# Store of the gated values, places of the early down chunks, and order of work in the tail of a Fourier mixing and GEGLU kernel

## The chip, the cores and the metric

The kernel runs on one core of one Trainium2 chip. The metric is the device time of one execution in microseconds. The core has five instruction queues that run side by side and meet only through semaphores: PE (TensorE, matrix products), DVE (VectorE), ACT (ScalarE), POOL (GpSimd) and SP (SyncE, which here only issues DMA transfers). Each queue is worked through strictly in the order in which the kernel was written.

## The reference

Input x has 2048 rows of 448. Two blocks with residuals follow each other:

```python
h  = x + Re(DFT_seq(DFT_hidden(layernorm(x))))     # as products with cosine and sine matrices
g  = layernorm(h) @ w_gate                          # 448 -> 1792
u  = layernorm(h) @ w_up
h2 = h + (gelu(g) * u) @ w_down                     # 1792 -> 448
```

All inputs and outputs are float32.

## The kernel before

**Precision and products.** Every float32 operand is split into a high float16 half (ACT, `hi_part`, L108) and a low half, the rest (DVE, `lo_part`, L112 or L114). A product takes three float16 products: high by high, high by low, low by high. On top of that, two by two blocks are multiplied by Strassen's scheme with seven products instead of eight, so sums of blocks must be made before the split.

**Stages.** First come the Fourier products (up to about 340 us). Then 42 *units* of gate and up follow, one for each 128 columns of the hidden width and each block of rows: units 0 to 13 work on the first half of the rows (512-wide products), 14 to 27 and 28 to 41 on a quarter each (256-wide). From unit 14 on, the *down* product is woven in between. Down has 56 *chunks*: eight row parts p (0 to 7) of seven chunks n; chunk d is p = d // 7, n = d % 7. Each chunk is 21 products (seven of Strassen, three terms each) into the accumulators `acc_d[p]`. Units 14 to 41 hold chunks 0 to 41, one or two per unit (`COUNT`, L1375). Chunks 42 to 55 (p = 6 and 7) come after the last unit, in the *tail* (L1454 to L1496).

**A unit** (`GateUp`, L1027). PE does x1, z1, y1, x2, z2, y2, y3 into three PSUM banks X, Y, Z. DVE's `c12` reads Z behind z2; Z is then free for z1 of the next unit. ACT does the copies and the two GELUs; POOL multiplies one half of the gated values (L1104), and DVE makes the other half behind y3 (L1089). y3 of unit t-1 is done at the beginning of unit t. `store` (L1106) writes the gated values `hs` to memory (`hid_dram`): one store for each unit in units 0 to 13, one for each two units after that. `hs` has two buffers.

**Preparing a chunk.** `hid_load` (SP, L1127) brings the chunk's gated values back, into one of six buffers; it waits on SP until the store that wrote them has landed. `dn_sums` (POOL, L1174 and L1175) makes four Strassen sums, `dn_sum5` (DVE, L1179) the fifth, `dn_hi` (ACT) and `dn_lo` (DVE) the halves, each as one instruction for the 256 raw columns and one for the 640 columns of sums. The first six products of a chunk need the raw part only. For a chunk of the next unit, load is two units ahead; sums are made at the end of the unit before, the rest in the unit ahead of its use.

**Early chunks.** Eight chunks of the tail (42, 49, 43, 50, 44, 51, 45, 52: n = 0 to 3 of p = 6 and 7) are prepared inside the units; `EARLY` (L1133) maps a unit t to a chunk. Its load is in unit t-1, `dn_sums` at the end of t-1, `dn_sum5` and `dn_hi` in t, `dn_lo` in t+1. Chunks 42 and 49 use what units 28 and 29 stored, 43 and 50 units 30 and 31, 44 and 51 units 32 and 33, 45 and 52 units 34 and 35. The other six chunks (46, 47, 48, 53, 54, 55) are prepared in the tail, in the order of the list `jit` (L1461).

**Drain** (L926). When the seven chunks of a part p have been added up, ACT copies two banks (`copy`, L940), DVE adds the two others (`bank2`, `bank3`, L944), POOL does the eight sums of the copies (`sums`, L972), and SP stores the rows (`dn_store`, L1237). Part 6 has its accumulators in the banks X, tr, Z, Y; part 7 uses bank X again for its seventh Strassen sum, so chunk 49 needs part 6's first bank to be copied.

**What sets the order.** It is written out by hand. Around the change: the loop of units 0 to 13 (L1286), the loop of units 14 to 41 (L1383), and the tail.

Of the kernel before, what the change touches and what calls it, by code (L numbers as in the profile page):

```python
# [16 lines left out]
NF = DF // P  # L17
# [15 lines left out]
def kernel(  # L33
# [76 lines left out]
    def lo_part(dst, src, hi, scale=1.0):  # L110
        if isinstance(scale, float) and scale == 1.0:
            V.tensor_sub(dst, src, hi)  # L112
        else:
            V.scalar_tensor_tensor(dst, src, scale, hi, op0=ALU.mult, op1=ALU.subtract)  # L114
# [873 lines left out]
    NC = NF // 2  # L988
# [127 lines left out]
    def gw_load(t):  # L1116
        gw[t] = w_tile(f"gw{t}")
        nc.sync.dma_start(gw[t], w_dram[f_of(t)])
# [4 lines left out]
    def hid_load(d):  # L1123
        p, n = divmod(d, NC)
        hid_in[d] = fpool.tile([P, 4, P], F32, tag="hid", bufs=6, name=f"hid{d}")
        b = max(p // 2 - 1, 0)
        nc.sync.dma_start(hid_in[d], hid_dram[b, n][:, p % 2 if b else p])  # L1127

    def dn_hid(d):
        return hid_in[d]  # L1130

    LAST = range(6 * NC, 8 * NC)
    EARLY = dict(zip((32, 33, 35, 37, 38, 39, 40, 41), (42, 49, 43, 50, 44, 51, 45, 52)))  # L1133

    def dn_places():
        home = {}
# [23 lines left out]
    def dn_sums(d):  # L1160
        t = dn_hid(d)
        if d in LAST:
            spare.append(d)
            s = fops.tile([P, 5, P], F32, tag=("xn", "tt")[len(spare) % 2], name=f"dn_s{d}")
        elif d % 4 < 2:
            if d % 4 == 0:
                opened["l"] = late.tile([P, 10, P], F32, tag="dn_s", name=f"dn_s{d}")
            s = opened["l"][:, d % 4 * 5 :][:, :5]
        else:
            if d % 4 == 2:  # L1170
                opened["s"] = prep.tile([P, 10, P], F32, tag="s", name=f"dn_s{d}")
            s = opened["s"][:, d % 4 % 2 * 5 :][:, :5]
        dn_s[d] = s
        G.tensor_add(s[:, 0:2], t[:, 0:2], t[:, 2:4])  # L1174
        G.tensor_sub(s[:, 2:4], t[:, 1:4:2], t[:, 0:4:2])  # L1175

    def dn_sum5(d):
        t = dn_hid(d)
        V.tensor_add(dn_s[d][:, 4], t[:, 0], t[:, 3])  # L1179

    def dn_parts(d):
        return (dn_hid(d)[:, 0:4:3], slice(0, 2)), (dn_s[d], slice(2, 7))
# [6 lines left out]
    def dn_lo(d):  # L1189
        for src, dst in dn_parts(d):  # L1190
            lo_part(dn_w[d][:, 1, dst], src, dn_w[d][:, 0, dst])
# [44 lines left out]
    def dn_store(p):  # L1236
        nc.sync.dma_start(outr[p // 4, p % 4], hr[p])  # L1237
# [46 lines left out]
    prev = None  # L1284
    PREP_AT = {0: 0, 1: 1, 3: 2, 5: 3, 7: 4, 9: 5, 11: 6}
    for t in range(NF):  # L1286
        w = gu.get(t + 2) if t + 2 in JIT_F else None
        n = PREP_AT.get(t)
        if t > 0 and w is None:
            gw_load(t + 2)  # L1290
        if t + 2 == NF:
            for d in (0, 1, 2):
                hid_load(d)
        if t + 1 == NF:
            hr_load(0)
        if prev:
            prev.y3()
        if w:
            w.sums()
        if t == NF - 1:  # L1300
            dn_sum5(0)
        cur.y1()
        if t == 3:

            gelu_table()
        if w:
            w.hi(True)
        if n is not None:
            down_hi(n, 0)
            down_lo(n, 0)  # L1310
        cur.x2()
        if n is not None:
            down_hi(n, 1)
        if w:
            w.hi(False)
            w.lo(True)
        cur.z2()
        do(t, 1)
        cur.y2()
        do(t, 2)  # L1320
        cur.c_last()
        if t == NF - 1:
            dn_hi(0)
        if t == 1:
            hid_mm(NP - 1, 0)
        prev, cur = cur, GateUp(t + 1)
        cur.x1()
        if w:
            w.lo(False)
            gw[t + 2] = w.w  # L1330
        if n is not None:
            for part in W_LO1:
                down_lo(n, 1, part)
        if t + 1 in PREP_AT and t > 0:
            down_sums(PREP_AT[t + 1])
        if t == 0:
            down_sums(1)
        if t == NF - 1:
            dn_lo(0)
        cur.z1()  # L1340
        if t == 1:
            hid_mm(NP - 1, 1)
            hid_add(NP - 1, 0)
            ffn_moments(NB - 1, 1, hp[NB - 1, 1], 0)
            hid.close()
            late = ctx.enter_context(tc.tile_pool(name="late", bufs=1, reuse_waits="tile"))
            hops_tile(2)
        if t == 2:
            hid_add(NP - 1, 1)
            ffn_moments(NB - 1, 1, hp[NB - 1, 1], 1)  # L1350
            h_store(NB - 1, 1)

            sd_last = root(moments[NB - 1, 1], "h_last")
        if t == 3:
            mv = moments[NB - 1, 1]
            moments[NB - 1, 1] = mv, rstd(mv, sd_last, "h_last", const)
        if t == NF - 2:
            dn_sums(0)
        if t == NF - 1:
            dn_sums(1)  # L1360
            dn_sums(2)
        do(t, 3)
        if t > 0:
            before.store()
        before = prev
        if w:
            w.store()
        if w and w.f + 4 in JIT_F:
            gu[w.f + 4] = Weights(w.f + 4)
        if n is not None and 2 <= n + 2 < NC:  # L1370
            down_load(n + 2)
        do(t, 4)
# [3 lines left out]
    steps, d = {}, 0  # L1376
# [5 lines left out]
    drains, ended = {}, {}  # L1382
    for t in range(NF, N_GU):  # L1383
        now, ahead = steps[t], steps.get(t + 1, [])
        extra = EARLY.get(t)
        if t + 2 < N_GU:
            gw_load(t + 2)
        far = steps.get(t + 2, []) + ([EARLY[t + 1]] if t + 1 in EARLY else [])
        far += [46] if t + 1 == N_GU else []
        for d in far:  # L1390
            hid_load(d)
        for d in ahead:
            if d % NC == 0:
                hr_load(d // NC)
        if t in (N_GU - 4, N_GU - 2):
            hr_load(6 + (t == N_GU - 2))
        dn_mm(now[0], range(0, 6))
        prev.y3()
        for d in ahead:
            dn_sum5(d)  # L1400
        if t - 1 in EARLY:
            dn_lo(EARLY[t - 1])
        if t in EARLY:
            dn_sum5(EARLY[t])
        cur.y1()
        cur.x2()
        dn_mm(now[0], range(6, 13 if len(now) == 1 else 21))
        for d in ahead:
            dn_hi(d)
        cur.z2()  # L1410
        do(t, 1)
        cur.y2()
        cur.c_last()
        for d in ahead[:1]:
            dn_lo(d)
        if len(now) == 1:
            dn_mm(now[0], range(13, 21))
        else:
            dn_mm(now[1])
        if now[-1] % NC == NC - 1:  # L1420
            p = now[-1] // NC
            ended[p], drains[p] = t, dn_drain(p)
            drains[p].copy()
        prev = cur
        if t + 1 < N_GU:
            cur = GateUp(t + 1)
            cur.x1()
        if now[-1] % NC == NC - 1:
            drains[p].bank2()
            drains[p].bank3()  # L1430
        if t + 1 < N_GU:
            cur.z1()
        for d in ahead[1:]:
            dn_lo(d)
        for d in far:
            dn_sums(d)
        if extra is not None:
            dn_hi(extra)
        do(t, 2)
        do(t, 3)  # L1440
        if t == NF:
            before.store()
        if NF < t and t % 2 == 0:
            before.store()
        before = prev
        do(t, 4)
        for p, t0 in ended.items():
            if p < 5 and t - t0 in (1, 2):
                n = 4 * (t - t0)
                drains[p].sums(range(n - 4, n))  # L1450
            if p < 5 and t - t0 == 3:
                dn_store(p)
# [3 lines left out]
    prev.store()  # L1456
    hid_load(48)
    dn_sum5(46)
    dn_lo(52)
    drain = drains[5]  # L1460
    jit = [46, 47, 48, 53, 54, 55]  # L1461
    for i, d in enumerate(range(6 * NC, 7 * NC + 4)):
        dn_mm(d)
        if jit:
            n = jit.pop(0)
            dn_hi(n)
            if jit:
                dn_sums(jit[0])
            dn_lo(n)
            if jit:  # L1470
                dn_sum5(jit[0])
            if len(jit) > 2:
                hid_load(jit[2])
            if i == 0:
                drain.sums(range(8))
                dn_store(5)
        if d == 7 * NC - 1:
            drain = dn_drain(6)
            drain.copy()
            drain.bank2()  # L1480
            drain.bank3()
            drain.sums(range(8))
            dn_store(6)

    drain = Drain(hr[7], (), (), 1.0 / (H_SC * W_SC))
# [71 lines left out]
```

## Time and profile before

| | |
|---|---|
| median of 3 runs | 719.24 us (718.64 to 721.21) |
| the profiled execution | 717.73 us, of it span from first to last instruction 716.0 us |
| TensorE clock granted | 1.000 |
| busy in the span | PE 704.2, DVE 522.1, ACT 355.5, POOL 201.9 us |
| DMA | 160.47 MB, mean 224 GB/s, 74.8% of 16 engines' time |
| unit 33 begins | 611.79 us |
| the tail's first chunk (42) begins | 679.51 us |
| PE's last product ends | 712.75 us |

A timeline row reads: start in us, duration in us, engine, line, operation, output<-inputs, shape and count of merged instructions, and in brackets how long the engine sat idle just before and what released it. A row of waits reads: waiting engine, tile and line, then what released it, us in total, times, longest. A row of a stretch reads: from:to, its length, and for PE, PE's weight loads, DVE, ACT and POOL the busy us with the count of instructions; then the clock, DMA's share and GB/s. A row of a group reads: line, engine, operation, count, and the shortest, median and longest duration in ns.

### The profile page before, as it was taken

The page shows a single profiled execution, that of the slowest core. Times are in us where ns is not written, and L with a number is a line of the kernel's source. Part 1 is how long each engine was busy: PE and PEld are TensorE (multiplying, and loading weights), DVE is VectorE, ACT ScalarE, POOL GpSimd, SP SyncE. Part 2 cuts the span into 40 slices and gives each one's busy share as a digit, 9 for nine tenths or more (in the row PEclk, how much of TensorE's full clock was granted, in tenths as well). Part 3 has the DMA queues.
Part 4 walks back from the last instruction along what each step waited for, and adds up shares of the span by engine and source line. Part 5 has one row for each costly group of instructions (what it writes and reads, how often), then busy time and mean ns, then how long its engine had stood idle before and what let it go on. Part 6 is the DMA issues. An engine that isn't in the chain of part 4 may idle for free.

```text
span 716.0 us, 13066 instructions
## 1 busy us (share of the span) xinstructions
PE 704.2 (98%) x4952; PEld 480.7 (67%) x4952; DVE 522.1 (73%) x1024; ACT 355.5 (50%) x656; POOL 201.9 (28%) x240
## 2 busy tenths in 40 slices
PE   9999999999999999999999999999999999999986
PEld 6555555555555555897644444469999999899986
DVE  7997638486858679998648777456777765978974
ACT  5776524162526444543527565455555544546530
POOL 0000000000000000000213333344485756678982
PEclk9999999999999999999999999999999999999999
DMA  7787629999998969652836858797798976879431
GB/s 270 248 248 263 146 104 243 232 310 246 225 308 245 250 212 238 238 136 91 222 123 204 314 188 194 225 293 244 219 287 267 274 253 208 295 252 321 165 116 51
DMA packets 116463, 160.47 MB, mean 224 GB/s; under 512 B 62000, under 2 KB 80560, under 8 KB 116400
## 3 DMA queue, kind: packets, MB, share of 16 engines
q1 hardware_dynamic: 116400, 159.64, 74.8%
q8 instruction: 38, 0.62, 0.3%
q14 instruction: 25, 0.20, 0.1%
HBM read 110.85 MB, written 34.87 MB: 204 GB/s over the span
## 4 chain that ended last, share of the span: by engine, by line
PE 92%; DVE 4%; POOL 1%; DMA 1%; issue 1%; ACT 0%; SPq 0%; ACTq 0%; POOLq 0%; DVEq 0%
PE acc L648 33%; PE pY L1010 13%; PE acc_d L1219 12%; PE y L714 9%; PE pX L1010 9%; PE pZ L1010 9%; PE acc_f L520 7%; DVE dn_w L112 1%; DMA hid_dram<-hs 1%; DVE dn_s L1179 1%; POOL hr L972 1%; PE pw L102 1%; DVE dn_l L112 0%; ACT dn_w L108 0%; DVE hr L944 0%
## 5 line engine op out<-in xcount | busy, mean ns | idle before, releaser
L648 PE MATMUL acc<-xs,ws 128*128 128x448 f16 x1248 | 237.9, 352 | 0.0
L648 PEld LDWEIGHTS <-ws 128*128 128x128 f16 x1248 | 122.1, 98 | 113.8
L1010 PEld LDWEIGHTS <-gw 128*128 128x128 f16 x1365 | 133.4, 98 | 44.6 <-issue 1.7
L1219 PE MATMUL acc_d<-wd,dn_w 128*128 128x224 f16 x1008 | 111.3, 259 | 2.9 <-DVE dn_w L112 2.3
L220 POOL TENSOR_TENSOR wd_s<-wd 128x448 f32<-128x448 f32 x7 | 9.5, 1352 | 343.4 <-DMA wd<-in_w_down_dram 342.6
L1219 PEld LDWEIGHTS <-dn_w 128*128 128x128 f16 x1008 | 96.6, 98 | 5.8 <-DVE dn_w L112 3.2
L1010 PE MATMUL pY<-hops,gw 128*128 128x256 f16 (+1 forms) x595 | 89.9, 294 | 0.0
L1104 POOL TENSOR_TENSOR hs<-hs,c 128x256 f32<-128x256 f32 (+1 forms) x42 | 47.5, 1131 | 127.6 <-DVE hs L1020 64.4
L114 DVE SCALAR_TENSOR_TENSOR ws<-wr,ws 128x1024 f16<-128x1024 f32 (+2 forms) x66 | 75.0, 1139 | 9.3 <-ACT ws L108 8.9
L108 ACT ACTIVATE ws<-wr 128x1024 f16<-128x1024 f32 (+2 forms) x66 | 63.8, 980 | 21.7 <-DMA wr<-in_w_seq_dram 20.5
L714 PE MATMUL y<-wh,z 128*128 128x448 f16 x336 | 66.2, 352 | 0.0
L1010 PE MATMUL pZ<-hops,gw 128*128 128x256 f16 (+1 forms) x385 | 61.7, 294 | 1.2 <-DVE c L1020 1.2
L1010 PE MATMUL pX<-hops,gw 128*128 128x256 f16 (+1 forms) x385 | 61.7, 294 | 0.0
L112 DVE TENSOR_TENSOR dn_w<-dn_s,dn_w 128x640 f16<-128x640 f32 x48 | 55.5, 1156 | 5.8 <-ACT dn_w L108 5.6
L1174 POOL TENSOR_TENSOR dn_s<-hid 128x256 f32<-128x256 f32 x56 | 45.4, 812 | 29.2 <-DMA hid<-hid_dram 27.9
L714 PEld LDWEIGHTS <-z 128*128 128x128 f16 x336 | 32.9, 98 | 30.1
L520 PEld LDWEIGHTS <-ws 128*128 128x128 f16 x504 | 48.3, 98 | 0.9
L1010 PEld LDWEIGHTS <-gu_w 128*128 128x128 f16 x273 | 26.6, 98 | 31.9 <-issue 0.2
L1066 ACT ACTIVATE u<-pY 128x256 f32<-128x256 f32 (+1 forms) x42 | 19.1, 455 | 57.6 <-PE pY L1010 57.5
L1175 POOL TENSOR_TENSOR dn_s<-hid 128x256 f32<-128x256 f32 x56 | 46.2, 826 | 0.0
L108 ACT ACTIVATE dn_w<-dn_s 128x640 f16<-128x640 f32 x48 | 35.1, 730 | 21.4 <-DVE dn_s L1179 10.1
L1089 DVE SCALAR_TENSOR_TENSOR hs<-pY,g 128x256 f32<-128x256 f32 (+1 forms) x42 | 21.3, 506 | 33.5 <-PE pY L1010 33.0
(133 smaller groups left out, 909.7 us busy)
## 6 DMA issues: line engine op xcount, KB each, us to landing
gw<-w_dram SPq DMA_DIRECT2D x35, 896.0 KB, 5.7
wr<-in_w_seq_dram SPq DMA_DIRECT2D x100, 256.0 KB, 4.7
hid_dram<-hs SPq DMA_DIRECT2D x28, 512.0 KB, 7.1
hid<-hid_dram SPq DMA_DIRECT2D x56, 256.0 KB, 5.9
w_dram<-gu_w SPq DMA_DIRECT2D x14, 896.0 KB, 5.4
gu_raw<-in_w_gu_dram SPq DMA_DIRECT2D x28, 384.0 KB, 5.9
wr<-in_w_seq_dram SPq DMA_DIRECT2D x14, 512.0 KB, 5.2
x<-in_x_dram SPq DMA_DIRECT2D x16, 224.0 KB, 2.9
```

The costliest lines, as they stand in the source:

```text
L108: A.activation(dst, src, AF.Copy, scale=scale)
L112: V.tensor_sub(dst, src, hi)
L114: V.scalar_tensor_tensor(dst, src, scale, hi, op0=ALU.mult, op1=ALU.subtract)
L520: PE.matmul(fast_sum(n, k), fast_a(n, i, lw, a), fast_b(j, lx, b), start=j == 0 and m == 0 and k % 2 == 0, stop=j == NT // 2 - 1 and m == ...
L648: PE.matmul(acc[key][:, :D], w[:, lw, block * P : (block + 1) * P], xs[c][:, lx, :], start=c == 0 and m == 0, stop=c == NT - 1 and m == 2,)
L714: PE.matmul(y[:, :D], z[p][:, lz, k, g * P : (g + 1) * P], wh[:, lw, k, :], start=k == 0 and m == 0, stop=k == 6 and m == 2,)
L1010: PE.matmul(ps, w[:, wl, wa + ws, :], ops[:, m + ms, :], start=first and n == 0, stop=last and n == len(terms) - 1, skip_group_check=True,)
L1089: V.scalar_tensor_tensor(h, y, SC, g, op0=ALU.mult, op1=ALU.mult)
L1104: G.tensor_mul(c22, c22, self.cols(self.c12))
L1174: G.tensor_add(s[:, 0:2], t[:, 0:2], t[:, 2:4])
L1175: G.tensor_sub(s[:, 2:4], t[:, 1:4:2], t[:, 0:4:2])
L1219: PE.matmul(ps, w[:, la, a, :], wd[n][:, lb, b, :], start=n == 0 and m == 0 and opens, stop=n == NC - 1 and m == 2, skip_group_check=True,)
```

## The change

Three things. The store of the gated values is issued right behind y3 and its product, at the beginning of the next unit, instead of near that unit's end. The eight early chunks are placed in units 32 to 39 without gaps. In the tail, low halves of chunk 52 are gone (they now fall into unit 40); the chunks still to be prepared are tied to the tail's iterations 0, 1, 2, 3, 7 and 8, with 54 and 55 behind drain 6's copy; drain 5's eight POOL sums are split into four in iteration 0 and four in iteration 2; the last three loads are all issued in iterations 0 to 2; drain 6's POOL sums and store move two iterations back.

```diff
-    EARLY = dict(zip((32, 33, 35, 37, 38, 39, 40, 41), (42, 49, 43, 50, 44, 51, 45, 52)))
+    EARLY = dict(zip(range(32, 40), (42, 49, 43, 50, 44, 51, 45, 52)))
...
@@ units 0 to 13
         if prev:
             prev.y3()
+            prev.store()
...
         do(t, 3)
-        if t > 0:
-            before.store()
-        before = prev
...
@@ units 14 to 41
         prev.y3()
+        if t % 2 == 0:
+            prev.store()
...
         do(t, 3)
-        if t == NF:
-            before.store()
-        if NF < t and t % 2 == 0:
-            before.store()
-        before = prev
...
@@ tail
     dn_sum5(46)
-    dn_lo(52)
-    drain = drains[5]
-    jit = [46, 47, 48, 53, 54, 55]
+    jit = {0: (46, 47), 1: (47, 48), 2: (48, 53), 3: (53, 54), 7: (54, 55), 8: (55, None)}
     for i, d in enumerate(range(6 * NC, 7 * NC + 4)):
         dn_mm(d)
-        if jit:
-            n = jit.pop(0)
+        if i in jit:
+            n, after_n = jit[i]
             dn_hi(n)
-            if jit:
-                dn_sums(jit[0])
+            if after_n:
+                dn_sums(after_n)
             dn_lo(n)
-            if jit:
-                dn_sum5(jit[0])
-            if len(jit) > 2:
-                hid_load(jit[2])
-            if i == 0:
-                drain.sums(range(8))
-                dn_store(5)
-        if d == 7 * NC - 1:
+            if after_n:
+                dn_sum5(after_n)
+        if i < 3:
+            hid_load(53 + i)
+        if i in (0, 2):
+            drains[5].sums(range(2 * i, 2 * i + 4))
+        if i == 2:
+            dn_store(5)
+        if i == NC - 1:
             drain = dn_drain(6)
             drain.copy()
             drain.bank2()
             drain.bank3()
+        if i == NC + 1:
             drain.sums(range(8))
             dn_store(6)
```

## The prediction, made before the changed kernel was run

> **What bounds the kernel now.** I read the page's busy times, then the waits of PE, then the order in time around each wait, then busy time by unit.
>
> ```profile
> span 716.0 us, 13066 instructions
> PE 704.2 (98%) x4952; PEld 480.7 (67%) x4952; DVE 522.1 (73%) x1024; ACT 355.5 (50%) x656; POOL 201.9 (28%) x240
> ...
> PE acc_d L1219 <- ACT v L940: 3.1, 1, 3.1
> PE acc_d L1219 <- DVE dn_w L112: 2.3, 2, 1.4
> ...
> PE pZ L1010 <- DVE c L1020: 1.2, 3, 0.6
> PE acc_d L1219 <- ACT dn_w L108: 0.4, 1, 0.4
> ```
>
> PE is the bound: 716.0 - 704.2 leaves 11.8 us in which it idles, and no reordering can return more. The four named waits shown make 7.0 us of that. Where they lie decides. The tail, in order of time:
>
> ```profile
> 679.51 4.19 PE L1219 MATMUL acc_d<-wd,hops 128*128 128x224 f16 x42
> ...
> 683.53 2.17 PE L1219 MATMUL acc_d<-wd,dn_l 128*128 128x224 f16 x21
> ...
> 684.52 6.02 POOL L972 TENSOR_TENSOR hr<-hr,v 128x224 f32<-128x224 f32 x8
> ...
> 691.93 0.74 ACT L108 ACTIVATE dn_w<-dn_s 128x640 f16<-128x640 f32 x1 [4.61 <-POOL dn_s L1175]
> ...
> 692.70 1.25 DVE L112 TENSOR_TENSOR dn_w<-dn_s,dn_w 128x640 f16<-128x640 f32 x1 [4.53 <-ACT dn_w L108]
> ...
> 694.00 1.42 PE L1219 MATMUL acc_d<-wd,dn_w 128*128 128x224 f16 x13 [0.91 <-DVE dn_w L112]
> ...
> 695.26 1.89 PE L1219 MATMUL acc_d<-wd,hops 128*128 128x224 f16 x18
> ...
> 699.00 0.74 ACT L108 ACTIVATE dn_w<-dn_s 128x640 f16<-128x640 f32 x1 [1.29 <-DVE dn_s L1179]
> ...
> 699.65 0.96 ACT L940 ACTIVATE v<-acc_d 128x448 f32<-128x448 f32 x2
> ...
> 700.22 0.45 PE L1219 MATMUL acc_d<-wd,hops 128*128 128x224 f16 x3 [3.08 <-ACT v L940]
> ...
> 706.55 6.20 PE L1219 MATMUL acc_d<-wd,dn_w 128*128 128x224 f16 x63
> ```
>
> Two chains. First, POOL adds all eight sums of drain 5 (6.02 us) before the two sums of chunk 48; ACT's high half and DVE's low half follow, and PE waits 0.40 + 0.91 us in chunk 48. Second, PE stops after 18 products of chunk 49, whose seventh sum goes into bank X; that bank is free only when drain 6's copy (699.65) has read it, and ACT does the copy behind the high half of chunk 55 (699.00). PE waits 3.08 us.
>
> Units 33 to 41 (rows: PE, PEld, DVE, ACT, POOL busy in a stretch that is one unit):
>
> ```profile
> 611.79:618.86 7.07, 6.44 (x63) 5.83 (x60) 6.93 (x15) 4.61 (x11) 5.19 (x7) 1.00 0.99 348
> ...
> 627.14:633.41 6.27, 6.27 (x62) 5.83 (x60) 4.39 (x8) 3.69 (x9) 6.27 (x10) 1.00 0.72 259
> ...
> 641.69:647.96 6.27, 6.27 (x62) 5.82 (x60) 4.55 (x8) 4.46 (x11) 5.04 (x7) 1.00 1.00 350
> ...
> 656.25:663.07 6.82, 6.43 (x62) 5.82 (x60) 5.50 (x10) 4.61 (x11) 6.74 (x10) 1.00 0.91 340
> 663.07:671.67 8.60, 8.44 (x83) 7.84 (x81) 8.60 (x12) 4.86 (x12) 8.60 (x10) 1.00 0.55 193
> 671.67:679.51 7.84, 7.69 (x77) 7.08 (x74) 7.78 (x12) 3.06 (x9) 6.83 (x8) 1.00 0.39 125
> ```
>
> A one-chunk unit takes 6.27 us undisturbed. Unit 33 takes 0.80 more, unit 39 0.55 more; unit 40 (two chunks: 21 products more, 6.27 + 2.01 = 8.28) 0.32 more, and unit 41 (42 products of down and, without x1 and z1 of a next unit but with its own y3, 32 of its own at 0.109: 7.52) 0.32 more, a hole at its head: 1.99 us in all. They are the units in which DVE or POOL has no room.
>
> **Part one: the earlier store.** A store on SP waits for its data and holds what is behind it, so SP's order counts. In the code, what lies between the old and the new place on SP is, unit by unit: nothing, except in unit 2, where the store passes the store of h. The transposes and dn_store stand behind the old place already; loads of gw, hid and hr ahead of the new one. So it is nearly the same queue. The one wait that a store causes shows why it stays:
>
> ```profile
> 462.70 8.74 SPq L306 DMA_TRANSPOSE hops<-xs  x3
> ...
> 472.65 0.54 SPq L1110 DMA_DIRECT2D hid_dram<-hs  x1
> ...
> 480.19 0.42 DVE L1020 SCALAR_TENSOR_TENSOR hs<-pY,m 128x256 f32<-128x256 f32 x1 [2.91 <-DMA hid_dram<-hs]
> ...
> 481.00 0.56 PE L1219 MATMUL acc_d<-wd,dn_w 128*128 128x224 f16 x4 [1.40 <-DVE dn_w L112]
> ```
>
> The store of unit 12 issues at 472.65 because three transposes from the end of iteration 12 hold SP to 471.4; both places of the store are in iteration 13, behind them. Price 0. Bounds: 0 and -1.40 (that wait gone). If unit 2's swap had no cover (PE idles nowhere there), it would cost one 0.5 us issue.
>
> **Part two: the tail.** PE does 14 chunks of 21 products = 294 from 679.51 to 706.55 + 6.20 = 712.75: 33.24 us. The first two rows give 42 in 4.02 (start to start): 0.0957 each, so 28.1, and 0.16 for the last to drain: 28.3. So 4.9 us can go: 4.39 of waits and about 0.5 of restarts. Does it? After, POOL does four of drain 5's sums (3.0 us) instead of eight before chunk 48, and copy 6 has only the high half of chunk 53 before it. Chunk 52's low half is no longer in the tail (two DVE instructions fewer at its head). What remains ahead of chunk 48 is a round trip through memory:
>
> ```profile
> 680.88 0.32 SPq L1114 DMA_DIRECT2D hid_dram<-hs  x1
> ...
> 684.21 0.79 SPq L1127 DMA_DIRECT2D hid<-hid_dram  x2
> ...
> DMA to landing us min/median/max: 2.7/3.4/3.8
> ...
> DMA to landing us min/median/max: 2.7/5.7/7.6
> ...
> DMA to landing us min/median/max: 3.0/7.0/8.1
> ```
>
> (The last rows, of the views by tile and by line: loads of hid from 670 on; loads of hid from 580 on; stores of hid from 590 on.) The store landed in 3.3 us, the load in 2.7: chunk 48 is there at 686.9, or 687.6 with the 0.7 us of part three. POOL has done sums 46, 47 and four of drain 5 by about 686. Then POOL 1.44, ACT 0.74, DVE 1.3: 691.1. PE asks for that half at 680.2 + 6 x 2.01 + 0.6 = 692.8: 1.7 us of slack. Copy 6: chunk 48 ends at 694.3, bank X is copied by 694.9, asked for at 696.0. Its eight POOL sums follow chunk 55's and end near 702, before PE's end at 708.5. Price -4.9; bounds -4.9 and, if 48's chain is late as now, -3.4 (the 3.08 and its restart alone).
>
> **Part three: early chunks in units 32 to 39.** Chunk 43 moves up by one unit, and 50, 44, 51, 45, 52 by two each. Nothing is added over all; the room changes. DVE works strictly in order: y3's product, fifth sums of the chunks ahead, low halves of the last early chunk, fifth sum of the new one, and only then c12, which frees bank Z for the next unit's z1. Unit 39 shows the whole list:
>
> ```profile
> 657.57 0.42 DVE L1089 SCALAR_TENSOR_TENSOR hs<-pY,g 128x256 f32<-128x256 f32 x1 [1.87 <-PE pY L1010]
> ...
> 661.95 0.41 DVE L1020 SCALAR_TENSOR_TENSOR c<-pZ,u 128x256 f32<-128x256 f32 x1
> ...
> 662.42 0.82 PE L1010 MATMUL pZ<-hops,gw 128*128 128x256 f16 x6 [0.39 <-DVE c L1020]
> ```
>
> y3 is ready 1.32 us into the unit; the list takes 4.38 to c12. z1 is the last 6 of 39 products of 0.109, due at 656.25 + 5.61 = 661.86, and starts 0.56 late. Now units 33 and 39 have this list with two chunks ahead (and 40). After, 33, 35, 37 and 39 have it: 0.80 + 3 x 0.5 = 2.3. Add a low half of the next chunk that comes late at a unit's head, as the 0.32 at unit 41, and copy 4 in unit 37 behind a late c12: 0.5 together. Units 40 and 41 lose their 0.64, since chunk 45's fifth sum and low halves leave them. 2.8 against 1.99: **+0.8**. Units 36, 38 and 40, with one chunk more of PE work, ask for c12 2.0 us later; walked through with the rows below, DVE reaches it 0 to 0.8 us in time.
>
> ```profile
> L1174 POOL TENSOR_TENSOR dn_s<-hid x26: 718/738/1306, 589.7 to 679.7; 128x256 f32<-128x256 f32 x26
> ...
> L1179 DVE TENSOR_TENSOR dn_s<-hid x25: 279/808/842, 592.6 to 677.4; 128x128 f32<-128x128 f32 x25
> L112 DVE TENSOR_TENSOR dn_w<-dn_s,dn_w x18: 810/1278/1352, 588.5 to 674.0; 128x640 f16<-128x640 f32 x18
> ```
>
> ```profile
> L112 DVE TENSOR_TENSOR dn_w<-hid,dn_w x26: 407/415/950, 581.2 to 698.8; 128x256 f16<-128x256 f32 x26
> ```
>
> These are the same instructions with and without POOL at work beside them: a pair of low halves is 1.22 or about 2.2 us. Bounds: -1.2 (only unit 33 still waits) and +2.1 (units 36 and 38 each late by one contended pair's extra 1.0 as well).
>
> Each early load now follows its store by one unit instead of up to three, and SP waits for the store's landing.
>
> ```profile
> 609.48 0.37 SPq L1114 DMA_DIRECT2D hid_dram<-hs  x1
> ```
>
> For chunk 43: 609.5 + 7.0 + 5.7 (the medians) = 622.2; DVE comes to it at 624.1. Behind the load on SP stand only hr and the next gw, due a unit later. At the longest of both (8.1 and 7.6), 625.2: 1.1 us of DVE, about what unit 34 has to spare before z1 of unit 35.
>
> **Sum.** 717.73 (its span 716.0 and 1.73 around it) - 4.9 + 0.8 + 0 = 713.6. The median shown, 719.24, lies 1.5 above the profiled execution; carried to it: 719.24 - 4.1 = **715.1**.
>
> [...]
>
> [...]
>
> **Rivals and chances.** Forecast (tail whole, units +0.3 to +1.5), 714.6 to 715.8: 0.50. Units cost nothing or gain (to -1.2), 713.1 to 714.6: 0.16; for it speaks DVE's idle in units 35 and 37 (4.39 and 4.55 of 6.27). DVE's lag carries over through unit 37's drain into 38 (+2.1 to +3), 716.4 to 717.3: 0.20; for it, six full units in a row. Chunk 48's round trip at the medians above (7.0 and 5.7 instead of 3.3 and 2.7): 6.7 later less 1.7 slack, 5.0 lost, 720.1: 0.05; against it the light traffic there. Full exclusion, 720.6: 0.04. Part one does reach SP's order and the 1.40 goes, 713.7: 0.05. That it does nothing is in the forecast.
>
> About 0.5% (3.6 us: below 715.6) is what a measurement of this kernel tells from no change, and the forecast lies only just outside. Faster: most of the first case, the second and the last, 0.58; slower by as much (above 722.8): 0.04; within: 0.38. Range 712.9 to 717.8; it leaves out the two slow cases and part of the carry-over.
>
> **What would show it.** Right: no wait of PE on ACT v, copy 6 straight behind chunk 48, POOL's drain 5 in two halves, PE's last product about 4 us earlier; PE waits on c12 in units 33, 35, 37, 39 of about 0.5; the 1.40 at 481 unchanged. Wrong: a wait on hid loads on DVE in units 34 to 38, a wait over 1 us in unit 38, or a stop in chunk 48.

## The result, and the profile after

| | before | after |
|---|---|---|
| median of five executions, in turn | 719.24 us (718.37 to 721.21) | 715.19 us (713.94 to 716.42) |
| the profiled execution | 717.73 us | 716.42 us |
| its span | 716.0 us | 714.6 us |
| its TensorE clock | 1.000 | 0.998 |
| first product of unit 32 | 605.52 us | 604.96 us |
| the tail's first product | 679.51 us | 683.09 us |
| units 32 to 41 | 73.99 us | 78.13 us |
| the tail, to PE's last product | 33.24 us | 28.34 us |

The ratio is 0.994, with an interval of 0.9917 to 0.9964: 4.05 us faster by the medians. The two profiled executions differ by only 1.3 us, since that of before was quicker than its five executions and that of after is the slowest of its own. Both have a reason, which the experiments found and the prediction had not seen.

The busy times of the changed kernel and what PE waited for:

```profile
PE 705.7 (99%) x4952; PEld 481.6 (67%) x4952; DVE 526.4 (74%) x1024; ACT 355.4 (50%) x656; POOL 203.3 (28%) x240
```

```profile
PE pZ L1010 <- DVE c L1020: 3.2, 4, 1.9
PE pw L102 <- POOL sign_t L93: 1.4, 1, 1.4
PE acc_d L1219 <- DVE dn_w L112: 1.1, 2, 0.9
```

The 3.08 us on ACT's copy are gone, and so is the stop in chunk 48. The waits on `c12` have grown from 1.2 to 3.2 us. The tail in order of time:

```profile
683.09 4.19 PE L1219 MATMUL acc_d<-wd,hops 128*128 128x224 f16 x42
...
684.62 0.32 SPq L1114 DMA_DIRECT2D hid_dram<-hs  x1
684.72 3.39 POOL L972 TENSOR_TENSOR hr<-hr,v 128x224 f32<-128x224 f32 x4
...
689.00 1.74 SPq L1127 DMA_DIRECT2D hid<-hid_dram  x4
...
691.14 6.20 PE L1219 MATMUL acc_d<-wd,dn_w 128*128 128x224 f16 x63
691.62 0.42 ACT L108 ACTIVATE dn_w<-hid 128x256 f16<-128x256 f32 x1 [3.19 <-DMA hid<-hid_dram]
...
694.16 1.25 DVE L112 TENSOR_TENSOR dn_w<-dn_s,dn_w 128x640 f16<-128x640 f32 x1 [1.39 <-ACT dn_w L108]
...
696.82 0.53 ACT L940 ACTIVATE v<-acc_d 128x448 f32<-128x448 f32 x1
...
697.18 2.18 PE L1219 MATMUL acc_d<-wd,hops 128*128 128x224 f16 x21
...
705.23 6.20 PE L1219 MATMUL acc_d<-wd,dn_w 128*128 128x224 f16 x63
```

PE works from 683.09 to 705.23 + 6.20 = 711.43 with no bracket behind any of its rows: 28.34 us, where 28.3 was forecast. The copy (696.82) is done before chunk 49, from 697.18 on, asks for its bank. Chunk 48 is a closer call. Its low half is complete at 694.16 + 1.25 = 695.41; PE comes to the sums part of it at 697.18 - 2.01 + 0.6 = 695.77. That is 0.36 us of slack.

The units cost more than forecast. Rows of units 33 to 41 (columns as in the prediction's rows of stretches; the last three of a row are clock, DMA share and GB/s):

```profile
611.23:618.25 7.02, 6.43 (x63) 5.82 (x61) 6.88 (x15) 4.62 (x11) 5.21 (x7) 1.00 0.95 351
618.25:626.53 8.28, 8.28 (x84) 7.84 (x81) 8.28 (x12) 3.92 (x10) 6.12 (x8) 1.00 0.85 270
626.53:633.29 6.76, 6.43 (x63) 5.82 (x60) 5.59 (x10) 4.58 (x11) 6.76 (x9) 1.00 0.80 285
633.29:641.96 8.67, 8.45 (x83) 7.77 (x81) 8.67 (x12) 3.96 (x10) 8.67 (x11) 1.00 0.42 129
641.96:650.46 8.50, 6.60 (x62) 5.75 (x60) 6.75 (x12) 5.00 (x12) 6.17 (x8) 1.00 0.94 331
650.46:660.48 10.02, 9.95 (x83) 8.71 (x81) 8.67 (x16) 4.55 (x12) 6.50 (x8) 0.83 0.85 284
660.48:667.29 6.81, 6.42 (x62) 5.82 (x60) 5.49 (x10) 4.61 (x11) 6.38 (x10) 1.00 0.85 292
667.29:675.58 8.29, 8.29 (x84) 7.83 (x82) 8.29 (x12) 4.87 (x12) 8.29 (x10) 1.00 0.31 123
675.58:683.09 7.51, 7.51 (x76) 7.16 (x74) 4.08 (x8) 2.96 (x7) 2.33 (x4) 1.00 0.41 131
```

Units 40 and 41 lost their lateness, as the prediction had it (8.29 and 7.51 against its 8.28 and 7.52). Units 33, 35 and 39 are 0.5 to 0.75 over 6.27, unit 36 is 0.39 over 8.28. Two are far off. Unit 37 is 8.50 instead of 6.27. Unit 38 is 10.02 instead of 8.28, and PE is *busy* in 9.95 of it, at a mean clock of 0.83. What led to both, in order of time:

```profile
633.48 4.05 POOL L972 TENSOR_TENSOR hr<-hr,v 128x224 f32<-128x224 f32 x4
...
637.55 0.39 SPq L1237 DMA_DIRECT2D out_dram<-hr  x1
...
638.03 0.42 SPq L1118 DMA_DIRECT2D gw<-w_dram  x1
...
638.54 1.88 SPq L1127 DMA_DIRECT2D hid<-hid_dram  x3
...
644.69 0.29 DVE L1179 TENSOR_TENSOR dn_s<-hid 128x128 f32<-128x128 f32 x1 [0.97 <-DMA hid<-hid_dram]
...
645.76 0.63 DVE L1179 TENSOR_TENSOR dn_s<-hid 128x128 f32<-128x128 f32 x1 [0.78 <-DMA hid<-hid_dram]
...
649.65 0.81 PE L1010 MATMUL pZ<-hops,gw 128*128 128x256 f16 x6 [1.90 <-DVE c L1020]
...
651.21 2.55 PE L1010 MATMUL pY<-hops,gw 128*128 128x256 f16 x11
```

SP stands at the store of drain 3 (L1237) until POOL has finished that drain's sums, at 637.5. Behind it in SP's queue are the weights of unit 38 and three loads: chunks 35 and 36, which unit 38 uses, and the early chunk 51. Before, the same store went out 2.27 us sooner:

```profile
631.79 3.46 POOL L972 TENSOR_TENSOR hr<-hr,v 128x224 f32<-128x224 f32 x4
...
635.28 0.39 SPq L1237 DMA_DIRECT2D out_dram<-hr  x1
```

So in unit 37 DVE finds the two chunks not yet landed and stands 0.97 + 0.78 = 1.75 us. `c12` follows late by about as much, and z1 of unit 38 waits 1.90 us. About 1.3 us after that wait the clock falls to half:

```profile
649.50:652.00 2.50, 2.28 (x16) 1.81 (x16) 2.47 (x6) 2.37 (x7) 1.12 (x3) 0.80 0.85 296
652.00:654.00 2.00, 2.00 (x12) 1.39 (x11) 1.90 (x5) 0.55 (x2) 2.00 (x3) 0.50 0.50 99
654.00:656.00 2.00, 2.00 (x20) 1.87 (x19) 2.00 (x5) 1.20 (x4) 1.50 (x2) 0.90 0.88 358
```

The three rows lack 2.50 x 0.20 + 2.00 x 0.50 + 2.00 x 0.10 = 1.7 us of full clock: 3.4 us at half. y1 of unit 38, eleven products, takes 2.55 us there and 1.36 elsewhere. The account of the profiled pair closes: 0.56 us less up to unit 32 (most of it the wait near 480, now 0.89 instead of 1.40), 4.14 more in units 32 to 41, 4.90 less in the tail, 0.08 less behind PE: 1.4 less in the span.

### The profile page after: what moved, and what is told of

It is laid out like the page before. It is cut to its first block, busy times and chain, and to the rows that moved or that the text cites. A ratio compares the mean times of both kernels' runs of the same rounds, so it can differ in the third digit from the quotient of the medians.

```text
span 714.6 us, 13070 instructions
## 1 busy us (share of the span) xinstructions
PE 705.7 (99%) x4952; PEld 481.6 (67%) x4952; DVE 526.4 (74%) x1024; ACT 355.4 (50%) x656; POOL 203.3 (28%) x240
## 4 chain that ended last, share of the span: by engine, by line
PE 93%; DVE 3%; DMA 2%; issue 1%; ACT 0%; SPq 0%; POOL 0%; POOLq 0%; DVEq 0%
PE acc L648 33%; PE acc_d L1219 14%; PE pY L1010 13%; PE y L714 9%; PE pZ L1010 8%; PE pX L1010 8%; PE acc_f L520 7%; DMA hid_dram<-hs 1%; DMA hid<-hid_dram 1%; DVE dn_s L1179 1%; DVE dn_w L112 1%; PE pw L102 1%; DVE hops L112 0%; DVE dn_l L112 0%; ACT dn_w L108 0%
## 5 line engine op out<-in xcount | busy, mean ns | idle before, releaser
L1104 POOL TENSOR_TENSOR hs<-hs,c 128x256 f32<-128x256 f32 (+1 forms) x42 | 45.8, 1091 | 129.7 <-DVE hs L1020 81.9
L1174 POOL TENSOR_TENSOR dn_s<-hid 128x256 f32<-128x256 f32 x56 | 48.1, 859 | 30.5 <-DMA hid<-hid_dram 30.5
L1175 POOL TENSOR_TENSOR dn_s<-hid 128x256 f32<-128x256 f32 x56 | 45.8, 817 | 0.0
L972 POOL TENSOR_TENSOR hr<-hr,v 128x224 f32<-128x224 f32 x56 | 45.3, 835 | 0.6
```

Source lines behind the costliest of these rows:

```text
L972: op(x, x, m)
L1104: G.tensor_mul(c22, c22, self.cols(self.c12))
```

## The experiments

My theory: the tail brings the gain by two separate chains (chunk 48's sums on POOL, the copy on ACT); the earlier store brings nothing; the new places of the early chunks cost time, because DVE comes late to `c12` in the units with a full list and because SP is held in unit 36. The rivals: the earlier store carries some of the gain; the copy alone makes the tail; the cost of the places is spread evenly and has nothing to do with SP. Each kernel was run in turn with the kernel before, whose median beside them lay at 719.13 to 719.76 us. e1 to e4 ran on one chip, e5 to e8 on a second, e9 to e12 on a third, so between these groups the ratios are the better comparison.

| kernel | median, us | ratio to before | interval |
|---|---|---|---|
| e1: tail alone | 713.43 | 0.9912 | 0.9894 to 0.9930 |
| e2: early places alone | 719.36 | 0.9997 | 0.9984 to 1.0010 |
| e3: store alone | 719.23 | 1.0001 | 0.9986 to 1.0017 |
| e4: changed kernel, drain's rows stored a unit later | 714.16 | 0.9930 | 0.9911 to 0.9949 |
| e5: changed kernel again | 714.55 | 0.9932 | 0.9914 to 0.9950 |
| e6: e1, two transposes later | 716.98 | 0.9963 | 0.9946 to 0.9979 |
| e7: early chunks in even units, two more in the tail | 722.57 | 1.0036 | 1.0020 to 1.0052 |
| e8: e1, copy behind 54 and 55 | 720.65 | 1.0010 | 0.9999 to 1.0021 |
| e9: e1, one transpose later | 712.52 | 0.9904 | 0.9887 to 0.9921 |
| e10: e1, early chunks spread | 713.39 | 0.9920 | 0.9905 to 0.9936 |
| e11: e9 and e10 | 713.25 | 0.9910 | 0.9892 to 0.9928 |
| e12: e1, drain 5's sums in one piece | 715.19 | 0.9953 | 0.9934 to 0.9971 |

**The three parts, each alone.** e1 is the kernel before with the tail of the changed one. Chunk 52 is still early in unit 41 there, so its low halves stay at the tail's head.

```diff
     dn_lo(52)
-    drain = drains[5]
-    jit = [46, 47, 48, 53, 54, 55]
+    jit = {0: (46, 47), 1: (47, 48), 2: (48, 53), 3: (53, 54), 7: (54, 55), 8: (55, None)}
...
-        if d == 7 * NC - 1:
+        if i == NC - 1:
```

> The kernel before with the new tail alone; chunk 52's low halves go first in the tail, since its early unit stays 41. Theory (the tail gives all of the gain, the early places cost): PE waits nowhere in the tail, 28.3 us from its first to its last product instead of 33.2, units as before; about 714.4, not slower than the changed kernel. Rival (the new tail needs the new early places, since chunk 52's low halves hold DVE at its head and chunk 48 comes late again): PE waits over 1 us in chunk 48, 716 or more.

PE's waits in e1:

```profile
PE acc_d L1219 <- DVE dn_w L112: 1.6, 1, 1.6
PE pZ L1010 <- DVE c L1020: 1.5, 3, 0.7
...
PE acc_d L1219 <- ACT v L940: 0.2, 1, 0.2
```

None of these lies in the tail: the 1.6 is at 481, the others in the units. The tail runs from 680.76 to 709.10, 28.34 us as in the changed kernel. The tail alone brings 6.0 us by the medians, more than the whole change; the two intervals (0.9894 to 0.9930 and 0.9917 to 0.9964) overlap.

e2 has only the new places. Chunk 52's low halves leave the tail's head, since they belong to unit 40 there.

```diff
-    EARLY = dict(zip((32, 33, 35, 37, 38, 39, 40, 41), (42, 49, 43, 50, 44, 51, 45, 52)))
+    EARLY = dict(zip(range(32, 40), (42, 49, 43, 50, 44, 51, 45, 52)))
...
-    dn_lo(52)
```

> The kernel before with the new early places alone (so without chunk 52's low halves in the tail). Theory: the early places cost; PE waits about 2 us on c12 in unit 37, with 3.4 us at half clock in a part of the executions; the tail keeps its waits of 0.4, 0.9 and 3.1; 720.0 to 723. Rival (the early places cost nothing, the wait in unit 37 comes of the earlier store): 719.2 or less, unit 37 waits under 0.6.

It came out level, below the 720.0 to 723 that I had expected. Units 32 to 41 take 76.17 us, 2.2 more than before, with the `c12` waits of the changed kernel (0.67, 0.28, 1.52 and 0.16). But the waits in chunk 48 fall from 1.31 to 0.28, since DVE has two instructions fewer at the tail's head. I had left that out of the expectation. The trace before shows how it reaches chunk 48: POOL stood for chunk 52's low half before it could begin chunk 47's sums, and so came to drain 5's sums later.

```profile
682.45 0.84 POOL L1174 TENSOR_TENSOR dn_s<-hid 128x256 f32<-128x256 f32 x1 [1.30 <-DVE dn_xs L112]
```

In e2 that wait of POOL is gone. The old copy's wait is still there, and what follows it was new to me:

```profile
700.77 0.45 PE L1219 MATMUL acc_d<-wd,hops 128*128 128x224 f16 x3 [3.02 <-ACT v L940]
701.06 5.85 PE L1219 MATMUL acc_d<-wd,dn_l 128*128 128x224 f16 x42
```

42 products that take 4.19 us elsewhere take 5.85 here: the half clock again, 1.7 us, behind the 3.02 us wait. The profiled execution of the kernel before had the same wait and kept its clock.

e3 has only the earlier store (the two places of `before.store()` removed, `prev.store()` behind y3 in both loops).

```diff
             prev.y3()
+            prev.store()
...
-        if t > 0:
-            before.store()
```

> The kernel before with the earlier store alone. Theory: SP's order differs in one place, so 719.2 within 1 us and the wait near 480 stays at 0.9 to 1.4. Rival (the earlier store does matter): over 1 us faster or slower, or that wait gone.

No difference, and the wait near 481 is 1.39 us (before: 1.40). The store brings nothing that the interval of about 1 us either way can show, and the rival that it carries a good part of the gain is out.

**SP in unit 36.** e4 is the changed kernel with the store of a drained part one unit later, so that it no longer stands ahead of the loads. e5 is the changed kernel once more, on another chip than e4.

```diff
-            if p < 5 and t - t0 == 3:
+            if p < 5 and t - t0 == 4:
                 dn_store(p)
```

> The changed kernel with the store of a drained row part one unit later (parts 0 to 4). Theory (that store holds SP until POOL has done drain 3's sums, so the loads of chunks 35 and 36 go out about 4 us late, DVE waits for them in unit 37, c12 and PE follow, and the clock drops): unit 37's wait falls from 1.9 to 0.3 to 0.6, no stretch at half clock; 3 us less than the changed kernel's profiled execution, 712.5 to 714.0 in the median. Rival (DVE's list of work alone makes the wait, or the load of chunk 45 behind its store's landing): the wait stays above 1.2.

> The changed kernel itself, beside the others on one chip. Theory (its early places cost about 2 us against the tail alone): 714.5 to 716, a stretch of 3.4 us at half clock behind unit 37's wait in about half of the executions. Rival (the two were only measured on different chips): 713.4, as the tail alone.

In e4 SP gets to the loads 2.3 us sooner, and DVE makes both fifth sums without a wait:

```profile
636.23 1.56 SPq L1127 DMA_DIRECT2D hid<-hid_dram  x3
...
644.44 1.41 DVE L1179 TENSOR_TENSOR dn_s<-hid 128x128 f32<-128x128 f32 x2
...
649.10 0.81 PE L1010 MATMUL pZ<-hops,gw 128*128 128x256 f16 x6 [0.55 <-DVE c L1020]
```

How late SP comes to the loads, counted from the first product of unit 36, and what followed, in five profiles (us):

| profile | unit 36 begins | the three loads go out | later by | DVE waits for them in unit 37 | z1 of unit 38 waits |
|---|---|---|---|---|---|
| before | 633.41 | 636.28 | 2.87 | 0 | 0 |
| after | 633.29 | 638.54 | 5.25 | 1.75 | 1.90 |
| e2 | 633.52 | 638.78 | 5.26 | 1.64 | 1.52 |
| e5 | 634.49 | 638.47 | 3.98 | 0.45 | 0.34 |
| e4 | 634.17 | 636.23 | 2.06 | 0 | 0.55 |

DVE's wait goes with SP's lateness, in e2 with the store of the gated values at its old place too, and it is gone where the drained rows no longer stand ahead of the loads. So the mechanism is right: SP's order makes DVE's wait. But e5, the unaltered changed kernel, shows that the 1.90 is not in every execution: there POOL began the six sums ahead of the drain's 0.68 us earlier against PE, the drain's four took 3.46 us instead of 4.05, and z1 waited 0.34 us. Why POOL was quicker no run tells. So z1's 0.55 in e4 against the 1.90 of after does not by itself show a gain in time, and the ratios (0.9930 and 0.9932) show none; e4's median lies just above what I had expected. What is left are four short waits on `c12` in units 33, 35, 37 and 39: 0.97, 0.49, 0.55 and 0.55 in e4, 0.69, 0.49, 0.34 and 0.15 in e5, both at a clock of 1.000. Units 32 to 41 take 75.75 us in e4 and 75.29 in e5, against 78.13 in the profile of after.

**The two chains of the tail.** e8 is e1 with chunks 54 and 55 prepared in iterations 4 and 5, ahead of drain 6's copy. e12 is e1 with drain 5's eight sums in one piece.

```diff
-    jit = {0: (46, 47), 1: (47, 48), 2: (48, 53), 3: (53, 54), 7: (54, 55), 8: (55, None)}
+    jit = {0: (46, 47), 1: (47, 48), 2: (48, 53), 3: (53, 54), 4: (54, 55), 5: (55, None)}
```

> The tail alone, but chunks 54 and 55 prepared in iterations 4 and 5 as before, ahead of drain 6's copy on ACT. Theory (the 3.1 us are ACT's copy behind the high halves of 54 and 55, and a hole of that length drops the clock to half for 3.4 us in a part of the executions): PE waits 2 to 3 us in chunk 49, 2.5 to 4 us more than the tail alone, 716 to 717.5, granted clock below 1 in some executions where the tail alone has none. Rival (the copy waits because chunk 48 came late, so the split of drain 5's sums alone cures it): no wait in chunk 49, 713.4.

```diff
-        if i in (0, 2):
-            drains[5].sums(range(2 * i, 2 * i + 4))
-        if i == 2:
+        if i == 0:
+            drains[5].sums(range(8))
             dn_store(5)
```

> The tail alone, but drain 5's eight POOL sums in one piece in iteration 0, as before; chunks 54 and 55 stay behind drain 6's copy. Theory (two separate chains: the copy's place cures the 3.1 us in chunk 49, the split of the sums cures the 1.3 us in chunk 48): PE waits 0.8 to 1.8 us in chunk 48, none in chunk 49, 1 to 2 us more than the tail alone, ratio to the kernel before 0.993 to 0.9945. Rival (the split does nothing by itself): no wait in chunk 48, ratio about 0.991.

The rows of e8, then those of e12:

```profile
680.45 4.19 PE L1219 MATMUL acc_d<-wd,hops 128*128 128x224 f16 x42
...
699.56 0.74 ACT L108 ACTIVATE dn_w<-dn_s 128x640 f16<-128x640 f32 x1 [1.27 <-DVE dn_s L1179]
700.20 0.96 ACT L940 ACTIVATE v<-acc_d 128x448 f32<-128x448 f32 x2
...
700.78 0.72 PE L1219 MATMUL acc_d<-wd,hops 128*128 128x224 f16 x3 [4.35 <-ACT v L940]
701.29 6.17 PE L1219 MATMUL acc_d<-wd,dn_l 128*128 128x224 f16 x42
```

```profile
692.21 0.36 PE L1219 MATMUL acc_d<-wd,dn_w 128*128 128x224 f16 x2 [0.42 <-ACT dn_w L108]
693.50 1.42 PE L1219 MATMUL acc_d<-wd,dn_w 128*128 128x224 f16 x13 [0.92 <-DVE dn_w L112]
```

In e8 chunk 48 has no wait, ACT reads the bank only behind chunk 55's high half, and PE waits 4.35 us, again with half clock behind (42 products in 6.17 us). I had expected 2 to 3 us. The difference is that PE comes to chunk 49 sooner by the 1.31 us that it no longer stops in chunk 48: 3.08 + 1.31 = 4.39. It goes on at 700.78, 20.33 us behind the tail's first product; before, that was 700.22 - 679.51 = 20.71. So with the copy left late, the split gains only 0.4 us of order. With the half clock on top, e8 is 7.2 us behind e1 (I had expected 2.5 to 4): the gain of the tail is gone, and a little more. In e12 the waits are in chunk 48 alone, 0.42 + 0.92, and it is 1.8 us behind e1 by the medians, 2.9 by the ratios. So there are two chains, and the copy's is the longer one. The first costs its 1.3 us only once the copy is in its new place; until then curing it mostly moves the wait to chunk 49. That the copy alone makes the tail is out too.

**The wait near 481.** Three transposes hold SP there, for 8.74 us from 462.70 on in the trace before. e6 moves the last one of both halves of the second quarter to a later place; e9 moves that of the second half only, behind the store.

```diff
-                lambda q=q, j=j: ffn_transpose(q, j, (2, 3)),
+                lambda q=q, j=j: ffn_transpose(q, j, (2,)),
+                lambda q=q, j=j: ffn_transpose(q, j, (3,)),
```

> The tail alone (places of the early chunks and of the store as before), and in units 10 and 13 the last of the four transposes of a quarter's operands behind the store of the gated values, so that the store of unit 12 goes out one transpose earlier. Theory (that store's place behind three transposes makes the wait near 480): the store issues near 469.5 instead of 472.6, the wait of 0.7 to 1.6 goes, 1 to 1.5 us less than the tail alone, 712.2. Rival (the store's landing is set by the traffic, or the transpose delays what follows): the wait stays or moves, 713.4 or more.

```diff
+            if (q, j) == (2, 1):
+                plan = plan[:-1] + (lambda q=q, j=j: ffn_transpose(q, j, (2,)),)
+                at(side, (NF - 1, 4), lambda q=q, j=j: ffn_transpose(q, j, (3,)))
```

> The tail alone, and only the last transpose of the second half of a quarter (unit 12) moved behind the store of unit 12 in iteration 13. Theory (in the run with both halves moved, the wait in unit 11 came of the first half's transpose, which still held the buffer xs when ACT wanted it; the second half's does not): no wait near 453, none or under 0.4 near 480, 1 to 1.5 us less than the tail alone, ratio to the kernel before about 0.990. Rival (moving a transpose always costs what it saves): 0.992 or more.

In e6 the wait near 481 is gone, but there is a new one 28 us earlier:

```profile
450.91 0.83 ACT L108 ACTIVATE xs<-xn_h 128x256 f16<-128x256 f32 x2 [6.67 <-DMA hops<-xs]
...
452.79 2.56 PE L1010 MATMUL pY<-hops,gw 128*128 128x512 f16 x6 [3.14 <-ACT pY L1055]
```

The buffer `xs` exists once. The first half's late transpose still reads it when ACT wants to write the second half's part into it; ACT stands 6.67 us, and the copy that PE needs is queued behind. Moving the first half as well was my mistake. e9 leaves it alone: 0.53 us near 481 (I had expected under 0.4), no wait at 453, and the lowest median of all. Against e1 that is 0.9 us, which the intervals don't separate.

**Other places for the early chunks.** e7 puts them into the units with two chunks (and 41), leaves 51 and 52 to the tail, and takes e6's transposes and e4's store along. e10 is e1 with seven early chunks spread out and 52 left to the tail. e11 is e9 and e10 together.

```diff
-    EARLY = dict(zip((32, 33, 35, 37, 38, 39, 40, 41), (42, 49, 43, 50, 44, 51, 45, 52)))
+    EARLY = {32: 42, 34: 43, 36: 44, 38: 45, 40: 49, 41: 50}
...
+    jit = {0: (46, 47), 1: (47, 48), 2: (48, 51), 3: (51, 52), 4: (52, 53), 5: (53, 54), 7: (54, 55), 8: (55, None)}
```

> The tail and the transposes as in the run before, and the early chunks 42, 43, 44, 45, 49 in the units 32, 34, 36, 38, 40 and 50 in 41; 51 and 52 are prepared in the tail; the row parts' stores one unit later. Theory (c12 is late where a unit has two chunks ahead and both the low halves and the fifth sum of an early one): units 33, 35, 37, 39 miss the fifth sum and PE waits under 0.3 in each, the tail has room for two chunks more: 1 to 1.5 us less than the run before, 711. Rival (the tail then has too much for DVE and POOL, or chunk 48 comes late): PE waits over 1 us in chunks 46 to 52, 713 or more.

```diff
-    EARLY = dict(zip((32, 33, 35, 37, 38, 39, 40, 41), (42, 49, 43, 50, 44, 51, 45, 52)))
+    EARLY = {32: 42, 34: 43, 35: 49, 36: 44, 38: 45, 40: 50, 41: 51}
...
+    jit = {0: (46, 47), 1: (47, 48), 2: (48, 52), 3: (52, 53), 7: (53, 54), 8: (54, 55), 9: (55, None)}
```

> The tail alone, and the early chunks in units 32, 34, 35, 36, 38, 40 and 41 (42, 43, 49, 44, 45, 50, 51); 52 is prepared in the tail's iteration 3, and 53, 54, 55 in 7, 8, 9, behind drain 6's copy. Theory (c12 is late only where two chunks ahead meet both halves of an early chunk's work): units 33, 37 and 39 have no wait above 0.3, unit 35 about 0.5, no wait above 0.5 in the tail; 1 us less than the tail alone, ratio about 0.990. Rival (chunk 55 late for the last loop, or the wait only moves): a wait over 1 us behind 690, 0.992 or more.

> Both of the two runs before together: if the two gains are separate waits, they add: ratio about 0.9875, 2 to 2.5 us less than the tail alone; if one hides the other, no less than the better of the two.

In e7 no unit waits on `c12` any more, which is what the theory of the full list says. The rest went wrong: the copy now stands behind chunk 53's high half on ACT (4.12 us of wait in chunk 49), and the transposes' wait at 453 is 3.76. e10 shows the same for the units without these two. Its waits:

```profile
PE acc_d L1219 <- DVE dn_w L112: 1.2, 1, 1.2
PE pY L1010 <- ACT pY L1055: 1.1, 1, 1.1
PE acc_d L1219 <- ACT v L940: 0.5, 1, 0.5
PE pZ L1010 <- DVE c L1020: 0.4, 1, 0.4
```

One `c12` wait is left (unit 35, which still has an early chunk), the tail has none, and units 32 to 41 take 73.62 us. Yet the median is that of e1; the 1 us that I had expected does not show. e11 has a single wait of 0.73 us besides the one at the kernel's start, and a profiled span of 708.6 us, but its median is no better than e9's: the 2 to 2.5 us of two gains added up are not there. Its executions range from 710.34 to 714.06. What moves them I have not found; no run tells it.

## Why the prediction was right, and where it was not

The forecast of 715.1 us met 715.19. By the medians its two large terms were off in opposite directions, the tail at 6.0 us instead of 4.9, the places at 1.1 to 1.8 instead of 0.8, so the closeness is partly luck. On the profiled pair, for which the sum was worked out, it does not hold: 1.3 us were gained (717.73 to 716.42) where 4.1 were forecast, with the tail at -4.90 and the ten units at +4.14.

**Part one, price 0: right, to about 1 us.** That is what e3's interval tells. The wait at 481 is 0.68 to 1.39 us in four profiles with the earlier store and 1.15 to 1.64 in six with the later one and the same transposes, so the 0.89 of after need not be an effect of the store; e3, which changes nothing else, has 1.39.

**The tail, -4.9: right in the trace, too small for the medians.** 28.34 us against the 28.3 forecast, no wait on ACT, copy straight behind chunk 48, drain 5 in two halves; e8 and e12 show both chains. Chunk 48's slack was mis-sized: 0.36 us, not 1.7, counted alike (PE needs the low half two products later still, as the row of two in e12 shows). Its store took 4.4 us from issue to the moment at which SP could go on to the load (684.62 to 689.00), instead of 3.3, and the halves and sums behind came some tenths later as well. What the sum lacked is the clock. It started from the profiled execution before, and that was one that kept full clock through its 3.08 us hole. Most did not (next section but one). Without the hole the median gains more: 6.0 us in e1, of which 4.9 is in the order and the rest fits the half clock that is no longer there.

**The units, +0.8: sign right, too small.** Against e1 the whole change costs 1.1 us by e5 and 1.8 by the first measurement (1.4 and 2.0 by the ratios). The intervals overlap, but the eleven executions lie at 713.94 to 717.34 us and the six of e1 at 711.57 to 714.37, so the sign is likely and the size open. By profile the ten units take 1.3 us (e5), 1.8 (e4), 2.2 (e2) or 4.1 (after) more than before. Two terms made it:

- "0.80 + 3 x 0.5" for the units with the full list: borne out by e4 (2.56 in the four units, where 2.3 was forecast) and by e7 and e10, in which the units without a full list do not wait; e5 has less, 1.67. Units 40 and 41 lost their 0.64 as forecast.
- "Behind the load on SP stand only hr and the next gw": this is the step that failed. It looked at what is behind the loads and not at what is ahead. The store of drain 3 stands ahead and waits for POOL, and POOL comes later: it begins the six sums in front of the drain's 0.97 us later than before, they take 5.02 us instead of 4.30, and the drain's four 4.05 instead of 3.46. The forecast gave the loads 1.1 us of DVE at most, in unit 34; they cost 1.75 in unit 37 of that profile, and the clock another 1.7 (1.64 without a loss of clock there in e2, 0.45 in e5). I had named "a wait on hid loads on DVE in units 34 to 38" as a sign that it is wrong, and it was there.

**The rivals.** DVE's lag carried over into unit 38 (+2.1 to +3) came near in size and is wrong in kind: `c12` of unit 38 is done at 657.25, z1 has no wait there, and the 10.02 us are the clock. Full exclusion, 720.6 among the chances, is shown by no run: in unit 40 the low halves and fifth sums of DVE and the ten instructions of POOL would add to about 11 us (an estimate, 3 x 1.22 + 2 x 0.28 + 10 x 0.72, from the shortest durations in the prediction's rows); they ran in 8.29, and PE never waits there. The store's gain of 1.40 is not in e3: its ratio is 1.0001 and the wait is still there. Units that cost nothing exist (e10), but not with these places.

**Chances and range.** Faster by over 0.5% had 0.58, and 0.994 is just that side of the bound, as the forecast was. The interval, 0.9917 to 0.9964, reaches over the bound, so which side it is on is not settled.

## What to carry to other kernels

When work is moved on a queue that waits in order, look at what stands ahead of it as well as behind: here a store of finished rows that waited for POOL held back loads which DVE needed 6 us later. When two chains end at neighbouring waits, curing the shorter one may only move its wait to the other. A wait of PE of 3 us or more, and in one case of 1.9, has to be priced with the half clock that may follow (it did in 24 of 32 executions with a wait of 3.0 to 3.1 us), so a profiled execution that kept its clock understates what removing the wait is worth. And when a change bundles a gain with a cost, try the gain alone: by the medians the tail by itself beats the whole change.

## What the runs showed of the hardware that I had not expected

TensorE's clock falls to half behind a hole in PE's work, for about 3.4 us or twice that. By rows of two microseconds from 700.5 to 706.5, 1.7 us of full clock are missing in e2 (clock 0.74, 0.50, 0.90) and 2.4 in e8 (0.50, 0.50, 0.79), where the fall began earlier: its mean clock of 0.995 in a span of 718.7 us is about 3.6 missing in all. 3.4 us at half in a 716 us span is a mean clock of 0.9976, twice that 0.995. Of the kernel before, 70 executions ran beside the experiments: 20 kept a clock of at least 0.999, with a median of 717.9 us; 50 did not, 719.9 us. Of these 50, 27 read 0.998 and 12 read 0.995; the other 11 read 0.997, which this count does not give. The kernel has one hole of about 3 us, in chunk 49; that the clock fell there is seen in profiles such as e2's and only taken to be so in the rest. e2, e3 and e6, with a hole of 3.0 to 3.1 us, lost clock in 24 executions of 32, e8 (4.35 us) in all 12, e7 (3.76 and 4.12 us) in all 12, down to 0.990. e1, e4, e9, e10 and e12, whose longest wait from the units on is 1.64 us, kept 1.000 in all 29; e11, with 0.73 us, reads 0.999 in three of six. In between lies the changed kernel: 1.90 us in its profile, with half clock; 0.69 in that of e5, without; its eleven executions show both.

When the clock falls differs too: 1.3 us after the wait in the changed kernel, 0.7 us after it in e2, and before it is over in e8, where the clock is 0.50 all the way from 700.5 to 702.5 and PE waits until 700.78.

The half clock is also why two profiles of one kernel can differ by 2 us (717.9 and 719.9 by the medians above) without any change in its order of work: the mean clock beside the span, 0.998 against 1.000, is the first thing to look at.
